# Loading x and the transform matrices before the kernel stage, and taking the first norm's statistics inside it

## The chip, the cores and the metric

The program runs on one core of a Trainium2 chip. The metric is the device time of one execution in microseconds (us), the median of several runs. All data are float32; matrix products of the FFN use the fp32r format (a float32 operand rounded for TensorE) in a split into a high and a low part.

The engines are named as the profile names them: PE (TensorE matrix products), DVE (VectorE), ACT (ScalarE), POOL (GpSimd) and SP (SyncE, here only a queue that issues transfers). Each engine takes its instructions strictly in its own order, and waits on semaphores for the others.

## What is computed

One block of a network with adaptive layer norm (adaLN), a state-space convolution (S4D) and a ReLU feed-forward network (FFN), for 2048 positions of width 576, state size 128, FFN width 4608:

```
sa, ca, ga, sb, cb, gb = silu(c) @ w_mod          # six rows of 576
h  = layernorm(x) * (1 + ca) + sa
K[d, l] = 2 Re sum_n C[d, n] dt[d] exp((-exp(logA) + i A_imag) dt l)
x  = x + ga * (fft_convolution(h, K) + h * D_skip)
h  = layernorm(x) * (1 + cb) + sb
out = x + gb * (relu(h @ w1) @ w2)
```

## The kernel before

**Kernel stage (0 to about 171 us).** `KGen.first` makes the first 512 positions of the convolution kernel K, in six groups of 96 channels (`for g in range(NG)`). Per group ACT takes exponentials and sines of phases that PE made (`exps`, `turns`, `sines`), DVE and POOL build two tables, W2 (32 positions) and W1 (16 positions, by repeated doubling in `doubling`, line 256; the last doubling, m = 8, makes its products on DVE and its sums on POOL), and PE multiplies them (`products`, line 283: 192 small matmuls for each half u of the group, all through the helper of line 62). `rows` (line 325) copies a group's result out of PSUM into `ke` on ACT, and after groups 2 and 5 stores `ke` to DRAM (`kd`, line 403), one half of the channels (p = 0, 1) each. `mod` (line 549) runs between and makes the adaLN rows ga, ca, sa; their weights are loaded on SP at the start (lines 609, 610).

**Conv stage 0 (to about 250 us).** `main` (line 656) opens the pools of what follows and loads the transform matrices fcU, fcK, gc (line 665) on SP. `conv(0)` (line 833) loads x's first 512 rows (line 840), takes the layer norm (`norm1`, `stats`, `norms`: bn_stats, bn_aggr, Sqrt on ACT, reciprocal), and convolves in halves of 288 channels by odd-frequency transforms of length 1024 in four parts: PE multiplies with the matrices (`mm_K` of the kernel, `mm_U` of h; `transform`, line 736; `transform1`, line 774, for the kernel's second half), ACT evicts to Z, DVE does the butterflies (W, then K, U or V), the spectral products Y (`product`, with a temporary T), and PE the inverse (`inverse`, line 925, `ps_i`) added into x on DVE. `load_kt` (line 1023) loads the kernel back from `kd`; the skip term `dsk` is added to its first position (line 857). POOL's queue stores the spectra for later blocks (Rd and Kd of K, Ud of U; line 734). `mod_late` (line 624) makes the rows sb, cb, gb during this stage: for each a load of its weights into the one buffer `wm` on POOL's queue, 25 small matmuls (`mps_sb`, `mps_cb`, `mps_gb`), and for gb a way through DRAM.

**FFN (from about 250 us).** `ffn` (line 1032) runs 4 blocks of 512 positions, each 36 steps over slices of 128 of the FFN width. In block 0 the weights are split into high and low parts (line 1057, 1066 on ACT; 1059, 1069, 1070 on DVE), which are stored in DRAM for the other blocks. Between the matmuls a generator for each block is advanced by a hand-written budget (`step`, `rate`): in block 0 the rest of the kernel positions (`rest`) and conv(1), later conv(2) and conv(3).

**Order.** Python's order is the program's order, but the tile framework plans each engine's queue at build time and may move an instruction that is not marked `keep_in_program_order`. The helpers of `KGen` (`act`, `v`, `stt`, `pool`, `matmul`) mark theirs; the conv stage mostly doesn't. Pools are stacks of SBUF space; a tile in a later pool waits for the last users of the space that it takes over. The 13 transfers at the start and all of `kd`, `W1d`, `W2d`, `Zd` go through SP's queue in order.

Of the kernel before, what the change touches and what calls it, by code (L numbers as in the profile page):

```python
# [10 lines left out]
F32 = mybir.dt.float32  # L11
# [7 lines left out]
P = 128  # L19
# [21 lines left out]
class KGen:  # L41
# [31 lines left out]
    def setup(self, I):  # L73
# [8 lines left out]
        dt = self.pt.tile([P, D], F32, tag="T0", bufs=2, name="dt")  # L82
# [22 lines left out]
        def turn(h):  # L105
            th = self.pt.tile([KR, 4, P], F32, tag="T1", bufs=2, name="th")
# [149 lines left out]
    def doubling(self, g, i, u):  # L256
# [41 lines left out]
    def first(self, setup, mod):  # L298
# [42 lines left out]
        next(mod)  # L341
        turns = self.turns(0)
# [13 lines left out]
        for g in range(NG):  # L356
# [13 lines left out]
            run(double[2])  # L370
            if g + 1 < NG:
# [9 lines left out]
            if g > 0:  # L381
                rows(g - 1)
            run(*double[4:])
# [13 lines left out]
        run(late)  # L397
        return lambda: rows(NG - 1)
# [8 lines left out]
    def rest(self, psum, hs, blocks):  # L407
# [5 lines left out]
        with ExitStack() as ctx:  # L413
            pt = k.pool(ctx, f"kr{hs[0]}{blocks[0]}")
# [91 lines left out]
class Body:  # L506
# [3 lines left out]
    def build(self):  # L510
        nc, tc, I = self.nc, self.tc, self.I
        with ExitStack() as ctx:
# [13 lines left out]
            self.consts()  # L526
            kg = KGen(self)
            with ExitStack() as c2:
                kg.open(c2)
                setup = kg.setup(I)  # L530
                last = kg.first(setup, self.mod(kg))
            self.main(ctx, kg, last)

    def consts(self):
# [11 lines left out]
        self.dsk = c.tile([1, D], F32, name="dsk")  # L546
        nc.gpsimd.dma_start(out=self.dsk, in_=I["dsk"].unsqueeze(0))
# [76 lines left out]
    def mod_late(self):  # L624
# [3 lines left out]
        cb = self.cv.tile([P, 5, 32], F32, name="cb")  # L628
        nc.vector.tensor_copy(cb, self.ct.unsqueeze(2).broadcast_to([P, 5, 32]))
        for i, nm in ((3, "sb"), (4, "cb"), (5, "gb")):  # L630
            w = self.cv.tile([P, 5, D], F32, tag="wm", bufs=1, name=f"wm_{nm}")
# [4 lines left out]
            row = self.cv.tile([P, 2 * P], F32, tag="row", bufs=1, name=f"row_{nm}")  # L636
# [663 lines left out]
```

## Time and profile before

| | |
|---|---|
| time, median of 3 runs | 1431.17 us (1430.52 to 1433.48) |
| span of the profiled execution, first to last instruction | 1432.8 us |
| mean granted PE clock | 0.930 of full |
| PE busy | 1259.9 us (88%), 10720 instructions |
| DVE busy | 888.2 us (62%) |
| ACT busy | 491.2 us (34%) |
| POOL busy | 171.3 us (12%) |
| moved by DMA | 348 MB, 243 GB/s mean |
| first matmul of the FFN (line 1083) | 249.22 us |

A timeline row gives the start, the duration, the engine and line, the operation with the tile it writes and the tiles it reads, the shapes, how many instructions are merged, and in brackets how long the engine stood idle before it and what it waited for. "issue" means that it waited for nothing that the profile shows. A row with SPq or "DMA_DIRECT2D" is the issue of a transfer, not its duration. PE's ends are modelled, so a busy PE is not a PE at its peak.

### The profile page before, as it was taken

The numbers are of one execution on the slowest core, as the hardware profiler recorded it, in microseconds if no ns is written. First come the engines' busy times: TensorE is split into PE (matmuls) and PEld (weight loads), VectorE is DVE, ScalarE is ACT, GpSimd is POOL, SyncE is SP. The second block draws the span as 40 slices with busy tenths as digits, with TensorE's granted clock in tenths as the row PEclk, the third lists the DMA queues.
The fourth block names the chain that finished last, engine by engine and source line by source line (L and its number), as shares of the span: only waits on it lengthen the run. The fifth ranks groups of instructions, "written<-read, shape, count | busy, mean of one in ns | idle before, by whom it ended". The sixth has DMA issues, their size and how long they took to land. (4 is left out here: it accounts for less than half of the span.)

```text
span 1432.8 us, 26177 instructions
## 1 busy us (share of the span) xinstructions
PE 1259.9 (88%) x10720; PEld 994.5 (69%) x10720; DVE 888.2 (62%) x1332; ACT 491.2 (34%) x863; POOL 171.3 (12%) x279
## 2 busy tenths in 40 slices
PE   4665276999988997698999998999999999999997
PEld 2444155777876775476777776778787878888886
DVE  6889388999656678858836688563799532101112
ACT  4777042222221340151224322543332353323321
POOL 0667202000110100011010110010100000000000
PEclk9557588899999998899999999999999999999999
DMA  5647857576597694569867888585889657666662
GB/s 176 249 185 294 296 214 254 192 273 238 188 389 273 234 325 169 204 225 362 277 214 269 333 288 325 158 282 164 332 306 374 196 160 225 196 200 193 197 198 95
DMA packets 120268, 348.21 MB, mean 243 GB/s; under 512 B 23948, under 2 KB 24244, under 8 KB 109140
## 3 DMA queue, kind: packets, MB, share of 16 engines
q1 hardware_dynamic: 101044, 219.44, 46.9%
q0 software_dynamic: 18592, 125.73, 23.2%
q8 instruction: 84, 1.38, 0.4%
q10 hardware_dynamic: 512, 1.38, 0.3%
q14 instruction: 36, 0.29, 0.1%
HBM read 262.73 MB, written 83.76 MB: 242 GB/s over the span
## 5 line engine op out<-in xcount | busy, mean ns | idle before, releaser
L1083 PE MATMUL hps<-xh,w 128*128 128x512 f32 x1152 | 395.4, 402 | 0.0
L1109 PE MATMUL acc<-w,hh 128*128 128x512 f32 x1152 | 371.0, 404 | 8.7 <-DMA w<-L2d 5.7
L1089 DVE SCALAR_TENSOR_TENSOR hl<-hps,hh 128x512 fp32r<-128x512 f32 x144 | 99.0, 687 | 336.8 <-ACT hh L1088 336.5
L1109 PEld LDWEIGHTS acc<-w,hh 128*128 128x128 f32 x1152 | 217.3, 190 | 58.7 <-DMA w<-L2d 6.6
L1083 PEld LDWEIGHTS hps<-xh,w 128*128 128x128 f32 x1152 | 219.4, 191 | 48.2 <-ACT xh L1015 0.4
L1109 PE MATMUL acc<-w,hl 128*128 128x512 f32 x576 | 227.1, 406 | 8.6 <-DVE hl L1089 8.6
L1083 PE MATMUL hps<-xl,w 128*128 128x512 f32 x576 | 233.7, 406 | 0.0
L1088 ACT ACTIVATE hh<-hps 128x512 fp32r<-128x512 f32 x144 | 86.0, 597 | 361.7 <-PE hps L1083 348.3
L1066 ACT ACTIVATE w<-r 128x576 fp32r<-128x576 f32 x144 | 98.9, 687 | 261.3 <-issue 168.5
L1109 PEld LDWEIGHTS acc<-w,hl 128*128 128x128 f32 x576 | 109.6, 191 | 32.9 <-DVE hl L1089 9.5
L1083 PEld LDWEIGHTS hps<-xl,w 128*128 128x128 f32 x576 | 110.4, 192 | 23.6
L1057 ACT ACTIVATE w<-r 128x640 fp32r<-128x640 f32 x144 | 105.4, 732 | 28.4 <-DMA L1d<-w 23.8
L1083 PE MATMUL hps<-xs,w 128*128 128x512 f32 x288 | 99.7, 416 | 13.2 <-DMA w<-L1d 9.3
L62 PE MATMUL kps<-W,W 128*32 128x16 f32 x2304 | 45.6, 219 | 56.5 <-POOL W L59 33.1
L462 PEld LDWEIGHTS kps<-W1r,W2r 128*32 128x32 f32 x3456 | 68.0, 146 | 37.7 <-issue 27.8
L462 PE MATMUL kps<-W1r,W2r 128*32 128x48 f32 (+2 forms) x3456 | 78.3, 237 | 12.6 <-issue 10.2
L62 PEld LDWEIGHTS kps<-W,W 128*32 128x32 f32 x2304 | 40.7, 150 | 68.6 <-POOL W L59 36.1
L919 DVE TENSOR_TENSOR Y<-Y,T 128x1152 f32<-128x1152 f32 x64 | 84.6, 1349 | 0.0
L1083 PEld LDWEIGHTS hps<-xs,w 128*128 128x128 f32 x288 | 54.3, 192 | 27.9 <-DMA w<-L1d 11.0
L744 ACT ACTIVATE Z<-ps_f 128x288 f32<-128x288 f32 x120 | 48.2, 412 | 70.7 <-PE ps_f L743 63.6
L1109 PE MATMUL acc<-hh,w 128*128 128x512 f32 x144 | 58.1, 403 | 10.9 <-DVE w L1069 10.9
L1214 POOL DMA_DIRECT2D out_dram<-x x16 | 8.6, 544 | 463.3 <-DVE x L1206 461.4
(213 smaller groups left out, 1573.6 us busy)
## 6 DMA issues: line engine op xcount, KB each, us to landing
r<-in_w_dram SPq DMA_DIRECT2D x144, 320.0 KB
r<-in_w_dram SPq DMA_DIRECT2D x144, 288.0 KB, 3.4
w<-L1d SPq DMA_DIRECT2D x108, 320.0 KB, 3.8
w<-L2d SPq DMA_DIRECT2D x108, 288.0 KB
W2r<-W2d POOLq DMA_DIRECT2D x18, 1536.0 KB, 8.5
W2d<-W SPq DMA_DIRECT2D x12, 1536.0 KB, 8.6
Ua<-Ud POOLq DMA_DIRECT2D x15, 1152.0 KB, 10.1
W<-W1d POOLq DMA_DIRECT2D x18, 768.0 KB, 9.6
```

Source lines behind the costliest of these rows:

```text
L62: self.tc.keep_in_program_order(self.nc.tensor.matmul(*args, **kw))
L462: nc.tensor.matmul(ps[32 * dd : 32 * dd + 32, q, :], W2[:, r, :, ch], W1[:, :, r, ch], start=(r == 0), stop=(r == 1),)
L744: ev = nc.scalar.activation(Z[:, n2, c], ps[:, :PC], AF.Copy)
L919: v(y, y, T, op=op or ALU.add)
L1057: nc.scalar.activation(w[:, 0], r, AF.Copy)
L1066: nc.scalar.activation(w[:, 0:D], r, AF.Copy)
L1083: nc.tensor.matmul(ps, a, x, start=(i == 0), stop=(i == 13))
L1088: nc.scalar.activation(hh, ps, AF.Relu)
L1089: nc.vector.scalar_tensor_tensor(hl, ps, 0.0, hh, op0=ALU.max, op1=ALU.subtract)
L1109: nc.tensor.matmul(acc[i], a, x, start=(f == 0 and seen[i] == 1), stop=(f == NF - 1 and seen[i] == (3 if i < 4 else 2)),)
L1214: self.nc.gpsimd.dma_start(out=ov[:, n2], in_=x2[:, n2])
```

## The change

- `early` is new. Its first step loads x's first 512 rows, fcK, fcU and gc on SP right behind the adaLN weights of the start. Then, in groups 1 to 4 of the kernel stage, it takes the statistics of one of the four row sets each on DVE (two bn_stats and one bn_aggr, kept in order); in group 5 one Sqrt for all four on ACT (kept), and `moments`, a reciprocal and a product on DVE (not kept).
- `first` returns the second half of group 5's products and the last `rows` as separate pieces; `conv(0)` puts the transform of the kernel's first half (`mm_K(0)`) ahead of them, then `shift`, then the rows.
- `shift` replaces `norm1` in conv(0): ACT normalizes (Identity with scale and bias), then 1 + ca is multiplied and sa added, row set 3 on POOL, the others on DVE.
- The skip term of conv(0) is added on POOL.
- Pools: the kernel stage's lie on the right side of SBUF, the long-lived ones (x, matrices, FFN) on the left; T0, T1, t move from the pool `kg_t` to `kg_c`; conv 0 has a second pool `cvl` for its later tiles; the pools of `rest` and of the later conv stages are on the right too. PSUM pools are opened in the other order.
- fcKn and gcn are issued at step 36 in place of 40.

The core of the diff:

```diff
@@ -64,8 +64,8 @@
-        self.pa, self.pc, self.pt, self.pw = (pool(f"kg_{x}") for x in "actw")
-        self.ps, self.ph = pool("kg_ps", space=PSUM), pool("kg_ph", space=PSUM)
+        self.pt, self.pa, self.pc, self.pw = (pool(f"kg_{x}", side="right") for x in "tacw")
+        self.ph, self.ps = pool("kg_ph", space=PSUM), pool("kg_ps", space=PSUM)
...
@@ -267,10 +267,10 @@
-            t = self.pt.tile([P, 16 * H], F32, tag="T0", bufs=2, name="T0")
-            T = self.pt.tile([P, 16 * H], F32, tag="T1", bufs=2, name="T1")
+            t = self.pc.tile([P, 16 * H], F32, tag="T0", bufs=2, name="T0")
+            T = self.pc.tile([P, 16 * H], F32, tag="T1", bufs=2, name="T1")
-            t = self.pt.tile([P, 8 * H], F32, tag="t", bufs=2, name="t")[:, : 2 * n * m * H]
+            t = self.pc.tile([P, 8 * H], F32, tag="t", bufs=2, name="t")[:, : 2 * n * m * H]
@@ -339,6 +339,8 @@
         next(setup)
         next(mod)
+        early = k.early()
+        next(early)
         turns = self.turns(0)
         next(turns)
         next(setup)
@@ -368,6 +370,8 @@
             run(*double[:2])
             next(mod, None)
             run(double[2])
+            if 0 < g < 5:
+                next(early)
             if g + 1 < NG:
                 turns = self.turns(g + 1)
                 for _ in range(2):
@@ -380,6 +384,8 @@
                 run(late, double[3])
             if g > 0:
                 rows(g - 1)
+            if g + 1 == NG:
+                next(early)
             run(*double[4:])
             for u in range(2):
                 nc.sync.dma_start(
@@ -394,8 +400,9 @@
             run(a)
             if g + 1 < NG:
                 run(sines(g + 1))
-        run(late)
-        return lambda: rows(NG - 1)
+            else:
+                run(early)
+        return late, lambda: rows(NG - 1)
     def store(self, s, p, ke, eng):
...
@@ -524,12 +531,48 @@
             self.L1d = [dr.tile([P, 640], F32, name=f"L1d_{f}") for f in range(NF)]
             self.L2d = [dr.tile([P, D], F32, name=f"L2d_{f}") for f in range(NF)]
             self.consts()
+            self.x2, self.xT, self.ended = {}, {}, -1
+            self.dsk = self.cst.tile([1, D], F32, name="dsk")
+            nc.gpsimd.dma_start(out=self.dsk, in_=I["dsk"].unsqueeze(0))
+            self.sm = self.pool(ctx, "sm")
+            self.x2p = [self.pool(ctx, "x2a")]
             kg = KGen(self)
             with ExitStack() as c2:
                 kg.open(c2)
                 setup = kg.setup(I)
-                last = kg.first(setup, self.mod(kg))
-            self.main(ctx, kg, last)
+                late, last = kg.first(setup, self.mod(kg))
+            self.main(ctx, kg, late, last)
+
+    def early(self):
+
+        nc, I, sm = self.nc, self.I, self.sm
+        x2 = self.x2[0] = self.x2p[0].tile([P, 4, D], F32, tag="x2", bufs=1, name="x2_0")
+        nc.sync.dma_start(out=x2, in_=I["x"][0:512, :].rearrange("(m n) d -> m n d", n=4))
+        self.fcU, self.fcK, self.gc = (
+            sm.tile([P, 4, 2, P], F32, name=n) for n in ("fcU", "fcK", "gc")
+        )
+        for t, n in ((self.fcK, "fck"), (self.fcU, "fcu"), (self.gc, "gc")):
+            nc.sync.dma_start(out=t, in_=I[n])
+        kept = self.tc.keep_in_program_order
+        self.mv1 = mv = sm.tile([P, 4, 5], F32, name="mv1")
+        for i in range(4):
+            yield
+            st = sm.tile([P, 2, 6], F32, tag="st", bufs=8, name="st0")
+            for p in range(2):
+                kept(nc.vector.bn_stats(out=st[:, p], in_=x2[:, i, p * PC : (p + 1) * PC]))
+            kept(nc.vector.bn_aggr(out=mv[:, i, 0:2], in_=st))
+        yield
+        kept(nc.scalar.activation(mv[:, :, 2], mv[:, :, 1], AF.Sqrt, bias=self.eps))
+        yield
+        self.moments(mv)
+        yield
+
+    def moments(self, mv):
+
+        self.nc.vector.reciprocal(mv[:, :, 3], mv[:, :, 2])
+        self.nc.vector.scalar_tensor_tensor(
+            mv[:, :, 4], mv[:, :, 0], -1.0, mv[:, :, 3], op0=ALU.mult, op1=ALU.mult
+        )
     def consts(self):
         nc, I, c = self.nc, self.I, self.cst
...
@@ -625,15 +666,15 @@
-        cb = self.cv.tile([P, 5, 32], F32, name="cb")
+        cb = self.cvl.tile([P, 5, 32], F32, name="cb")
-            w = self.cv.tile([P, 5, D], F32, tag="wm", bufs=1, name=f"wm_{nm}")
+            w = self.cvl.tile([P, 5, D], F32, tag="wm", bufs=1, name=f"wm_{nm}")
-            row = self.cv.tile([P, 2 * P], F32, tag="row", bufs=1, name=f"row_{nm}")
+            row = self.cvl.tile([P, 2 * P], F32, tag="row", bufs=1, name=f"row_{nm}")
@@ -653,37 +694,32 @@
             self.tc.tile_pool(name=name, bufs=1, reuse_waits="tile", **kw)
         )
-    def main(self, ctx, kg, last):
+    def main(self, ctx, kg, late, last):
         nc, tc, I = self.nc, self.tc, self.I
-        self.sm = self.pool(ctx, "sm")
         for n, w in (("sb", 5), ("cb", 5), ("gb", D)):
             self.m[n] = self.sm.tile([P, w], F32, name=f"m_{n}")
-        self.fcU, self.fcK, self.gc = (
-            self.sm.tile([P, 4, 2, P], F32, name=n) for n in ("fcU", "fcK", "gc")
-        )
-        for t, n in ((self.fcU, "fcu"), (self.fcK, "fck"), (self.gc, "gc")):
-            nc.sync.dma_start(out=t, in_=I[n])
-        self.x2p = [self.pool(ctx, "x2a")]
         self.ff = self.pool(ctx, "ff")
         self.xp = [self.pool(ctx, "xa")]
-        self.x2 = {}
-        self.xT = {}
-        self.ended = -1
         with ExitStack() as c:
             self.cps = self.pool(c, "cps0", space=PSUM)
-            self.cv = self.pool(c, "cv0")
-            self.last_rows, self.nps = last, 4
-            self.fcKn, self.gcn = (self.cv.tile([P, 4, P], F32, name=n) for n in ("fcKn", "gcn"))
-            late = None
-            for i, _ in enumerate(self.conv(0)):
-                if i == 40:
+            self.cv = self.pool(c, "cv0", side="right")
+            self.cvl = self.pool(c, "cvl", side="right")
+            self.nps = 4
+            mods = None
+            for i, w in enumerate(self.conv(0)):
+                if w == "late":
+                    for _ in late:
+                        pass
+                elif w == "rows":
+                    last()
+                if i == 36:
                     for t, a in zip((self.fcKn, self.gcn), I["neg"]):
                         nc.gpsimd.dma_start(out=t, in_=a)
                 if i == 60:
-                    late = self.mod_late()
+                    mods = self.mod_late()
                 if i > 60 and i % 6 == 0:
-                    next(late, None)
-            for _ in late:
+                    next(mods, None)
+            for _ in mods:
                 pass
         self.nps = 1
         self.cps = self.pool(ctx, "cps", space=PSUM)
...
@@ -820,26 +854,44 @@
             yield from self.stats(
                 lambda i: x2[:, i, p * PC : (p + 1) * PC], [t[:, p] for t in st]
             )
-        rs = self.norms(st, kept)
+        rs = self.norms(st)
         yield 2.0
-        if kept:
-            self.last_rows()
         for i in range(4):
             mv = rs[i]
             f(h[:, i], x2[:, i], mv[:, 0:1], self.m["ca"], op0=ALU.subtract, op1=ALU.mult)
             f(h[:, i], h[:, i], mv[:, 3:4], self.m["sa"], op0=ALU.mult, op1=ALU.add)
             yield 1.6
+    def shift(self, x2, h):
+
+        nc, mv = self.nc, self.mv1
+        for i in (0, 2, 1, 3):
+            nc.scalar.activation(
+                h[:, i], x2[:, i], AF.Identity, scale=mv[:, i, 3:4], bias=mv[:, i, 4:5]
+            )
+        for i in (0, 2, 1, 3):
+            v = (nc.gpsimd if i == 3 else nc.vector).tensor_tensor
+            v(h[:, i], h[:, i], self.m["ca"], op=ALU.mult)
+            v(h[:, i], h[:, i], self.m["sa"], op=ALU.add)
+            yield 1.6
+
     def conv(self, s):
         nc = self.nc
         v = nc.vector.tensor_tensor
         xp = self.xp[s % 2]
-        x2 = self.x2p[s % 2].tile([P, 4, D], F32, tag="x2", bufs=1, name=f"x2_{s}")
-        self.x2[s] = x2
-        (nc.gpsimd if s else nc.sync).dma_start(
-            out=x2, in_=self.I["x"][s * 512 : (s + 1) * 512, :].rearrange("(m n) d -> m n d", n=4)
-        )
+        if s:
+            x2 = self.x2p[s % 2].tile([P, 4, D], F32, tag="x2", bufs=1, name=f"x2_{s}")
+            self.x2[s] = x2
+            nc.gpsimd.dma_start(
+                out=x2,
+                in_=self.I["x"][s * 512 : (s + 1) * 512, :].rearrange("(m n) d -> m n d", n=4),
+            )
+        else:
+            x2 = self.x2[0]
+            self.fcKn, self.gcn = (
+                self.cv.tile([P, 4, P], F32, name=n) for n in ("fcKn", "gcn")
+            )
         kt = [self.load_kt(s, 0), None]
         yield -1
         yield -1
@@ -854,7 +906,8 @@
             ktv = kt[p].rearrange("p (t dd g) q -> p t dd g q", t=2, g=2)
             if s == 0:
                 dv = self.dsk.rearrange("o (dd p q) -> o dd p q", dd=4, p=2)[:, :, p]
-                v(ktv[0:1, 0, :, 0], ktv[0:1, 0, :, 0], dv, op=ALU.add)
+                k0 = ktv[0:1, 0, :, 0]
+                nc.gpsimd.tensor_tensor(k0, k0, dv, op=ALU.add)
             src = lambda n2: ktv[:, n2 // 2, :, n2 % 2]
             if s == 0 and p == 1:
                 return self.transform1(src, self.fcK, self.fcKn, Z)
@@ -953,10 +1006,12 @@
         Us, Ks, Vs = [], [], []
         ZK, ZU = self.spec("Z"), None
         if s == 0:
-            yield from self.norm1(x2, h, True)
             yield from mm_K(0, ZK)
+            yield "late"
+            yield from self.shift(x2, h)
+            yield "rows"
         else:
-            yield from both(self.norm1(x2, h, False), mm_K(0, ZK))
+            yield from both(self.norm1(x2, h), mm_K(0, ZK))
         kt[1] = self.load_kt(s, 1)
         ZU = self.spec("Z")
         yield from both(spec_K(0, ZK), mm_U(0, ZU))
...
```

The built order of the changed kernel around the end of the kernel stage, each engine's own queue (names shortened, repeats merged; in the kernel before, the four Sqrt stood in the same place on ACT, and Rd, Kd of K_1 came after wm_cb on POOL):

```
ACT : ... ke (group 4) | table load | Sqrt | Z | h0 | Z Z Z | h2 | Z Z Z Z | h1 h3 | ke (group 5) | Z ...
DVE : ... T (group 5, first doubling) | reciprocal | W W | product of the moments | t T | W W | ... | T T T T |
      h0 h0 | W | h2 | W | h2 | h1 | W | h1 | W | K_0 | W W W W | U_0 | W W W W | T T | copy | six FFN splits |
      U_1 | Y_0 | V_0 | K_1 | x x | Y_1 ...
PE  : ... group 4 | group 5, u = 0 | mm_K(0) | group 5, u = 1 | mm_U(0) | mm_U(1) | mm_K(1) | inverse (one output) |
      mps_sb | inverse (three outputs) | mps_cb | mps_gb | second inverse ...
POOL: ... zs zs | fcKn gcn | four sums of group 5 | skip term | h3 h3 | Rd_0 Kd_0 | Ud_0 | skip term | wm_sb |
      Ud_1 | Rd_1 Kd_1 | wm_cb | wm_gb | gb's way through DRAM | rest: W, Z, W2 loads (x of conv(1) behind the third W)
SP  : ... wm_sa | x fcK fcU gc | ... | Zd Zd | kt | W1d W1d | r | kd kd | r r | kt | r ...
```

Further on the order of conv(1)'s DVE work in FFN block 0 differs: its bn_stats stand some 60 instructions earlier, ahead of the last kernel positions of `rest`, and in its first spectral product an `hl` (line 1089) stands between two of the steps where before it stood behind the inverse butterflies.

More of the change, by code (lines that the diff above doesn't have):

```diff
@@ L105, in turn @@
         def turn(h):
-            th = self.pt.tile([KR, 4, P], F32, tag="T1", bufs=2, name="th")
+            th = self.pc.tile([KR, 4, P], F32, tag="T1", bufs=2, name="th")
             dtb = dtT[:, h].unsqueeze(2).broadcast_to([KR, 4, P])
@@ L413, in rest @@
         with ExitStack() as ctx:
-            pt = k.pool(ctx, f"kr{hs[0]}{blocks[0]}")
+            pt = k.pool(ctx, f"kr{hs[0]}{blocks[0]}", side="right")
             def load(h):
@@ L545, in consts @@
         nc.gpsimd.dma_start(out=self.sgn, in_=I["sgn"])
-        self.dsk = c.tile([1, D], F32, name="dsk")
-        nc.gpsimd.dma_start(out=self.dsk, in_=I["dsk"].unsqueeze(0))
     def mod(self, kg):
@@ L694, in pool @@
         def pool(s):
-            self.cv = self.pool(self.cvs, f"cv{s}")
+            self.cv = self.cvl = self.pool(self.cvs, f"cv{s}", side="right")
         def block0():
@@ L725, in half @@
     def half(self, name):
-        return self.cv.tile([P, 4, PC], F32, tag="T", bufs=2, name=name)
+        return self.cvl.tile([P, 4, PC], F32, tag="T", bufs=2, name=name)
     def load(self, src, name):
@@ L792, in stats, with norms @@
             yield 0.45
-    def norms(self, st, kept):
+    def norms(self, st):
         nc = self.nc
@@ L800, in norms @@
             nc.vector.bn_aggr(out=mv[:, 0:2], in_=st[i])
-            sq = nc.scalar.activation(mv[:, 2:3], mv[:, 1:2], AF.Sqrt, bias=self.eps)
-            if kept:
-                self.tc.keep_in_program_order(sq)
+            nc.scalar.activation(mv[:, 2:3], mv[:, 1:2], AF.Sqrt, bias=self.eps)
             rs.append(mv)
@@ L813, in sums, with norm1 @@
         return [self.sm.tile([P, 2, 6], F32, tag="st", bufs=8, name=name) for _ in range(4)]
-    def norm1(self, x2, h, kept):
+    def norm1(self, x2, h):
         f = self.nc.vector.scalar_tensor_tensor
@@ L985, in conv @@
             )
-        rs = self.norms(st, False)
+        rs = self.norms(st)
         yield 2.0
-        h2 = [self.cv.tile([P, D + 64], F32, tag="h2", bufs=4, name="h2") for _ in range(4)]
+        h2 = [self.cvl.tile([P, D + 64], F32, tag="h2", bufs=4, name="h2") for _ in range(4)]
         for n2 in range(4):
```

5 lines of the change are left out of this document (2 added, 3 removed).

## The prediction

> **What bounds the kernel now.** I read the page first, then busy time by stretches, then the timeline from 125 to 260 us, then what PE waited for after that.
>
> ```profile
> 150.00:172.00 22.00, 6.64 (x382) 6.25 (x382) 0.40 (x2) 0.00 (x0) 4.80 (x7) 0.50 1.02 348
> 350.00:400.00 50.00, 50.00 (x563) 40.35 (x554) 31.29 (x39) 12.25 (x21) 6.85 (x13) 1.00 0.65 231
> 550.00:600.00 50.00, 37.50 (x132) 28.56 (x132) 38.91 (x55) 7.41 (x12) 2.63 (x5) 0.84 0.69 247
> 1200.00:1300.00 100.00, 100.00 (x443) 82.83 (x442) 12.88 (x20) 30.20 (x48) 1.88 (x4) 1.00 0.70 207
> ```
>
> Columns: stretch, its length, busy time of PE, PE weight loads, DVE, ACT, POOL, then the granted clock, DMA share, GB/s. Once the FFN runs, PE is nearly full (100 of 100 us late, 37.5 of 50 at worst), so a microsecond by which the FFN starts earlier is a microsecond of the end. Between 150 and 172 no engine works: DVE 0.4 us, PE 6.6, while the DMA engines are full at 348 GB/s. That hole is what the change aims at.
>
> ```profile
> 145.29 0.70 PE L62 MATMUL kps<-W,W 128*32 128x16 f32 x31 [1.86 <-issue]
> 149.62 0.30 PE L62 MATMUL kps<-W,W 128*32 128x16 f32 x2 [3.63 <-POOL W L59]
> 150.57 1.66 PE L62 MATMUL kps<-W,W 128*32 128x16 f32 x94 [0.66 <-POOL W L59]
> 156.02 2.14 PE L62 MATMUL kps<-W,W 128*32 128x16 f32 x127 [3.79 <-issue]
> 164.24 2.13 PE L62 MATMUL kps<-W,W 128*32 128x16 f32 x128 [6.08 <-issue]
> 170.44 0.70 PE L62 MATMUL kps<-W,W 128*32 128x16 f32 x33 [4.06 <-issue]
> 172.62 2.98 DVE L791 BATCH_NORM_STATS2 st<-x 128x6 f32<-128x288 f32 x8 [22.22 <-DMA x<-in_x_dram]
> 176.50 0.47 ACT L50 ACTIVATE ke<-kps 128x384 f32<-128x384 f32 x1
> 181.97 5.64 PE L743 MATMUL ps_f<-kt,fcK 128*128 128x288 f32 x16 [10.82 <-DVE kt L857]
> 187.45 2.83 PE L743 MATMUL ps_f<-h,fcU 128*128 128x288 f32 x11
> ```
>
> Three things end late: x (DVE waits 22.22 us), the last kernel products (PE done at 171.1, idle 13.9 us of that for nothing but the next instructions, about every 128 products), and the transform of K, which waits behind the norm on DVE.
>
> **The change, part by part.** *x and matrices early.* The four loads queue on SP behind wm_sa, the last adaLN weight of the start, long before their use. The 22.22 us wait goes. Fewer bytes are in flight after 150, so I price PE's idle at an instruction block at 2.0 us, near the 1.86 of the row at 145.29, with 3.8 to 6.1 as the other end. At the front the loads follow the weights in their queue; I cost them nothing.
>
> *Statistics in the kernel stage.* In each of four row groups two bn_stats and one aggregate, which I count as a third: 3 x 2.98/8 = 1.1 us of DVE, ahead of the wait shown here:
>
> ```profile
> 127.89 0.96 DVE L53 TENSOR_TENSOR k<-ph,k 128x768 f32<-128x768 f32 x1 [1.14 <-ACT k L50]
> ```
>
> 1.14 us of idle for ACT's k cover it: nothing. Without that cover it would be 4 x 1.1 = 4.5.
>
> *The moments.* This is the catch. The Sqrt follows ke of group 4 on ACT. The built order puts the reciprocal that reads it into DVE's doubling chain, right behind the first T.
>
> ```profile
> 140.88 0.36 DVE L53 TENSOR_TENSOR T<-W,Zp 128x192 f32<-128x192 f32 x1
> 141.28 0.42 DVE L53 TENSOR_TENSOR W<-t,T 128x96 f32<-128x96 f32 x2
> 146.06 0.49 ACT L50 ACTIVATE ke<-kps 128x384 f32<-128x384 f32 x1 [7.24 <-PE kps L62]
> 146.56 1.28 ACT L801 ACT_TABLE_LOAD   x1
> 146.63 3.54 DVE L53 TENSOR_TENSOR T<-W,Zp 128x768 f32<-128x768 f32 x4
> 148.57 3.88 POOL L59 TENSOR_TENSOR W<-T,T 128x384 f32<-128x384 f32 x4 [1.60 <-issue]
> 48.54 1.28 ACT L50 ACT_TABLE_LOAD   x1
> 49.83 0.81 ACT L50 ACTIVATE s<-k 128x768 f32<-128x768 f32 x1
> ```
>
> ke ends at 146.55, the table at 147.84, Sqrt near 148.1: DVE stands from 141.2 to 148.1. That is 6.9 us, with two small operations 7.2. Queued behind are all of group 5's doublings, POOL's last sums and the last products. POOL ends at 152.45 + 7.2 = 159.6.
>
> [...]
>
> *Kernel products and transform of K reordered.* PE starts at 149.62 + 7.2 = 156.8, ends the block of 94 at 159.4, idles 2.0, does the other 96 (1.7) until 163.1, then the K transform (5.64) until 168.8, whose kt now gets its skip term on POOL. Then 192 products of the second half, 3.4 us, and one more 2.0 idle (the other boundary passes under the transform): 174.1. ke follows at 174.2, 2.3 us before the old 176.50. The shift runs meanwhile on ACT, DVE and POOL. Its slowest part is row 3 on POOL, two 128x576 at 3.88/4 x 1.5 = 1.5 us each; ACT delivers it near 171, so it ends by 174. So the U transform starts at 174.1 in place of 187.45.
>
> [...]
>
> *DVE from there.*
>
> ```profile
> 192.25 0.75 DVE L757 TENSOR_TENSOR W<-Z 128x576 f32<-128x576 f32 x1
> 211.94 0.74 DVE L757 TENSOR_TENSOR V<-Y 128x576 f32<-128x576 f32 x1
> 217.06 0.44 DVE L771 TENSOR_TENSOR K<-Z 128x288 f32<-128x288 f32 x1
> 233.73 0.68 DVE L1070 TENSOR_TENSOR w<-r,w 128x512 fp32r<-128x512 f32 x1
> ```
>
> The first W of U needs four outputs, eight passes at 2.83/11 us and an eviction: some 2.8 us (an estimate), so 176.9. From that W to the first V took 19.7 us of full DVE. Now one skip sum leaves it (0.4, as wide as the row at 217.06), five more of the six first FFN weight splits move into it (at 0.68 each at most 3.4; two are an eighth as wide as the row at 233.73, so 2.2) with a small copy (0.3), and the second W pair waits some 0.4 for PE: 22.2, so V at 199.1 against 211.94 and K_1 done at 204.7 against 217.43. DVE is 12.7 us ahead.
>
> *What is late next: the adaLN weights.* They use one buffer, each load waiting for the products of the one before, and PE's second inverse transform is queued behind the third product.
>
> ```profile
> 210.41 0.77 POOL L609 DMA_DIRECT2D wm_cb<-in_w_mod_dram  x1 [5.92 <-PE mps_sb L619]
> 217.56 2.22 PE L619 MATMUL mps_cb<-wm_cb,cb 128*32 128x128 f32 x50 [1.13 <-DMA wm_cb<-in_w_mod_dram]
> 217.79 0.57 POOL L734 DMA_DIRECT2D Rd<-K  x1 [6.08 <-DVE K L771]
> 220.08 0.77 POOL L609 DMA_DIRECT2D wm_gb<-in_w_mod_dram  x1 [1.18 <-PE mps_cb L619]
> 230.03 3.86 PE L619 MATMUL mps_gb<-wm_gb,cb 128*32 128x128 f32 x50 [3.31 <-DMA wm_gb<-in_w_mod_dram]
> 233.82 5.32 PE L940 MATMUL ps_i<-V,gc 128*128 128x288 f32 x16
> 249.22 0.73 PE L1083 MATMUL hps<-xs,w 128*128 128x512 f32 x2 [1.54 <-ACT xf L1013]
> ```
>
> Before, wm_cb went out ahead of the stores Rd and Kd and took 7.1 us, and wm_gb behind them landed 12.2 us after Rd's issue. In the new order Rd and Kd of K_1 stand ahead of wm_cb on POOL, so wm_cb pays that 12.2 (and some 0.6, since mps_sb now runs after the first inverse output): 204.8 + 12.8 = 217.6. mps_cb takes 3.86 after such an idle (2.22 warm): 221.5. wm_gb 7.1: 228.7. mps_gb 3.86: 232.6. The second inverse starts at 232.7 against 233.82. With both products warm and mps_sb too it is 229.4. The stage gains 1.1 to 4.4; I take 1.2, the cold end, since PE idles over 4 us ahead of each and mps_gb was cold after 3.31. From there to 249.22 nothing changes: PE paces the tail.
>
> *Block 0 of the FFN.* conv(1)'s x now stands far earlier in POOL's queue, and its statistics on DVE ahead of idle like that at 475.31.
>
> ```profile
> 475.31 0.23 DVE L1069 TENSOR_TENSOR w<-r,w 128x64 fp32r<-128x64 f32 x1 [5.52 <-ACT w L1066]
> 482.40 2.97 DVE L791 BATCH_NORM_STATS2 st<-x 128x6 f32<-128x288 f32 x8
> 548.14 0.79 PE L1109 MATMUL acc<-hh,w 128*128 128x512 f32 x1 [6.24 <-DVE w L1069]
> 601.93 2.08 PE L1109 MATMUL acc<-w,hl 128*128 128x512 f32 x4 [8.64 <-DVE hl L1089]
> 265.07 0.53 POOL L421 DMA_DIRECT2D W<-W1d  x1 [19.55 <-DVE T L431]
> ```
>
> Some 3.4 us of DVE leave the busy stretch, and in the first product an hl now comes between its steps. PE stood 6.24 and 8.64 us for DVE there. The gain lies between 0 and 14.9; I take 3, near the work moved. The early load of that x sits in POOL's queue between two kernel loads, where POOL was waiting 19.55 us for DVE: nothing, or a few us without that slack.
>
> **Sum.** 1.2 + 3.0 = 4.2 less. The profiled execution spans 1432.8, which becomes 1428.6. The span is 1.6 above the median of the three runs, so the median 1431.17 becomes 1427.0.
>
> **Rivals.** (1) The wait is only swapped: the weights hold the second inverse to its old time and block 0 keeps its stalls (they hang on the length of the spectral products on DVE, which stays). 1430.5, within 0.2%. For it: the second product's order is unchanged. (2) The weights aren't late: PE warm and wm_cb shares the DMA engines with the stores instead of queueing behind them, 7.1 again. Then wm_cb lands at 214.8, mps_gb ends near 226.4, and the stage gains 7; with 3 from block 0, 1421. For it: the rows give 7.1 where a load runs alone; against it, the DMA engines had no room while Rd, Kd and wm_gb ran:
>
> ```profile
> 220.00:225.00 5.00, 4.79 (x20) 3.58 (x21) 3.56 (x5) 0.53 (x4) 1.30 (x2) 1.00 1.04 361
> ```
>
> (3) Slower: PE's idle at the instruction blocks stays at 3.8 to 6.1 as at 156 to 170, because W2d, W1d and kt still fill the queues. Then the products of the second half end 4 to 6 us after 174.1, and U, V, K_1 and the weights behind them follow one for one. It decides from 175.3 on, where the 1.2 us are used up; at 180 the stage loses 4.7, and without block 0's gain that is 1436. Against it: the gap was 1.86 before the loads began.
>
> **How the numbers follow.** Forecast 0.42 (own range 1423.5 to 1430), rival 1 0.22, rival 2 0.18, rival 3 0.18. A change under 0.2%, 2.9 us, can't be told from none: faster means below 1428.3, slower above 1434.0. Faster: 0.32 of the forecast's 0.42 and rival 2, 0.50. Same: 0.10, 0.20 of rival 1 and 0.02 of rival 3, 0.32. Slower: 0.02 of rival 1 and 0.16 of rival 3, 0.18. The range 1419 to 1436 holds rival 2 with room and rival 3 to its price.
>
> **What would show it.** A DVE wait of about 7 us for ACT's Sqrt near 141 us. PE's last kps product between 173 and 177. The first W of U near 177. wm_cb landing 10 us or more after its issue, PE waiting for wm_cb and wm_gb, and the second inverse at 230 to 234. First hps within 4 us of 249. PE stalls at the first product of conv(1) below 6 us. Wrong if the reciprocal doesn't wait, if the second inverse starts before 228 or after 236, or if block 0's length changes by more than 8 us.

## The result, and the profile after

| | before | changed |
|---|---|---|
| median, first comparison (9 runs each) | 1433.73 us | 1428.51 us, ratio 0.9969 (0.9954 to 0.9983) |
| median, second comparison (27 and 12 runs) | 1433.36 us | 1430.23 us, ratio 0.9980 (0.9961 to 0.9999) |
| span of the profiled executions | 1432.8, 1434.0, 1433.0 us | 1423.3, 1428.5 us |

The change makes the kernel faster by 3 to 5 us (5.2 and 3.1 between the medians; forecast 1427.0); both intervals end below 1, the second only just. The first profile of the changed kernel is the fastest of its nine runs, so its span alone would overstate the gain. The busy time by stretches, same columns as for before:

```profile
150.00:172.00 22.00, 13.81 (x407) 11.64 (x408) 13.86 (x22) 7.07 (x15) 7.19 (x7) 0.67 0.63 185
550.00:600.00 50.00, 35.64 (x135) 27.30 (x134) 38.08 (x51) 8.64 (x14) 2.63 (x5) 0.88 0.67 244
```

The hole at 150 to 172 us is in good part filled (DVE 0.40 to 13.86 us, PE 6.64 to 13.81) and the DMA engines have room there (share 1.02 to 0.63). What became of that shows in the timeline of the changed kernel:

```profile
147.31 0.18 DVE L572 RECIPROCAL mv<-mv 128x4 f32<-128x4 f32 x1 [6.57 <-ACT mv L565]
...
155.68 0.30 PE L62 MATMUL kps<-W,W 128*32 128x16 f32 x2 [10.58 <-POOL W L59]
...
160.16 1.66 PE L62 MATMUL kps<-W,W 128*32 128x16 f32 x96 [1.86 <-issue]
...
167.18 3.14 PE L62 MATMUL kps<-W,W 128*32 128x16 f32 x192
...
169.89 1.97 DVE L875 TENSOR_TENSOR h<-h,m_sa 128x576 f32<-128x576 f32 x1
...
170.24 8.05 PE L779 MATMUL ps_f<-h,fcU 128*128 128x288 f32 x32
...
171.32 1.80 POOL L875 TENSOR_TENSOR h<-h,m_sa 128x576 f32<-128x576 f32 x1
...
171.78 1.96 DVE L794 TENSOR_TENSOR W<-Z 128x576 f32<-128x576 f32 x1
...
176.48 0.75 DVE L793 TENSOR_TENSOR W<-Z 128x576 f32<-128x576 f32 x1
...
182.88 5.01 POOL L910 TENSOR_TENSOR kt<-kt,dsk 1x288 f32<-1x288 f32 x1
...
198.72 0.76 DVE L793 TENSOR_TENSOR V<-Y 128x576 f32<-128x576 f32 x1
...
206.15 0.77 POOL L650 DMA_DIRECT2D wm_cb<-in_w_mod_dram  x1 [0.50 <-PE mps_sb L660]
...
216.84 3.86 PE L660 MATMUL mps_cb<-wm_cb,cb 128*32 128x128 f32 x50 [6.04 <-DMA wm_cb<-in_w_mod_dram]
...
221.00 0.80 POOL L650 DMA_DIRECT2D wm_gb<-in_w_mod_dram  x1 [13.55 <-PE mps_cb L660]
...
227.33 3.86 PE L660 MATMUL mps_gb<-wm_gb,cb 128*32 128x128 f32 x50 [5.49 <-DMA wm_gb<-in_w_mod_dram]
...
231.12 6.64 PE L993 MATMUL ps_i<-V,gc 128*128 128x288 f32 x16
...
246.93 1.22 PE L1138 MATMUL hps<-xs,w 128*128 128x512 f32 x2 [1.54 <-ACT xf L1068]
```

The U transform starts 17.2 us earlier (187.45 to 170.24), the first V 13.2 us earlier (211.94 to 198.72), the second inverse only 2.7 us (233.82 to 231.12), the first FFN product 2.3 us. DVE's waits in this stage (line, tile, releaser: us, times, longest), which were 22.2 us for x before:

```profile
DVE x L998 <- PE ps_i L993: 15.6, 4, 13.9
DVE h L874 <- ACT h L869: 8.0, 1, 8.0
DVE mv L572 <- ACT mv L565: 6.6, 1, 6.6
```

Much of the wait was exchanged for three others: Sqrt, ACT's normalized rows, and the second inverse behind the adaLN weights.

### The profile page after: what moved, and what is told of

It is laid out like the page before. It is cut to its first block, busy times and chain, and to the rows that moved or that the text cites. A ratio compares the mean times of both kernels' runs of the same rounds, so it can differ in the third digit from the quotient of the medians.

```text
span 1423.3 us, 26160 instructions
## 1 busy us (share of the span) xinstructions
PE 1261.6 (89%) x10720; PEld 994.9 (70%) x10720; DVE 889.7 (63%) x1322; ACT 494.2 (35%) x864; POOL 180.8 (13%) x283
## 4 chain that ended last, share of the span: by engine, by line
PE 66%; DVE 10%; DMA 6%; issue 3%; ACT 1%; POOL 1%; SPq 0%; POOLq 0%; DVEq 0%; ACTq 0%
PE acc L1164 28%; PE hps L1138 27%; PE kps L469 4%; PE ps_f L779 3%; DMA w<-L2d 2%; PE ps_i L993 2%; DVE Y L972 2%; DVE T L970 2%; DVE T L438 1%; DMA L1d<-w 1%; DVE W1r L440 1%; DMA wm_cb<-in_w_mod_dram 1%; DVE W1r L444 1%; DMA Ua<-Ud 1%; DMA Ud<-U 1%
## 5 line engine op out<-in xcount | busy, mean ns | idle before, releaser
L1138 PE MATMUL hps<-xs,w 128*128 128x512 f32 x288 | 100.8, 419 | 10.3 <-DMA w<-L1d 3.2
```

The lines of the kernel that those rows point to most:

```text
L1138: nc.tensor.matmul(ps, a, x, start=(i == 0), stop=(i == 13))
```

## The experiments

The kernel stage ran up to 2.4 us apart in executions with the same order up to there, so the table counts from the first T of 768 columns of group 4 on DVE (110.67 to 113.38 us from the start). The expected texts give times from the start of the span, mostly on the clock of the changed kernel's first profile (112.98); where the difference decides between two theories, the text below says so. Blocks 1 to 3 run from the first output copy of block 0 to that of the last block. Ratios are against the kernel before, run beside each.

| kernel | first V | second inverse | first FFN product | block 0, us | blocks 1 to 3, us | ratio (95%) |
|---|---|---|---|---|---|---|
| before, 3 profiles | 98.6, 98.6, 99.6 | 120.4, 120.4, 121.3 | 135.8, 135.8, 137.1 | 372.6, 373.5, 374.5 | 798.9, 799.8, 797.4 | |
| changed, 2 profiles | 85.7, 86.3 | 118.1, 118.8 | 134.0, 134.0 | 372.3, 373.8 | 792.3, 795.9 | 0.9969, 0.9980 |
| moments kept | 84.9 | 117.0 | 131.2 | 373.8 | 791.8 | 0.9936 (0.9916 to 0.9956) |
| two buffers wm | 86.0 | 109.1 | 125.2 | 373.0 | 796.5 | 0.9891 (0.9874 to 0.9908) |
| both | 84.3 | 107.7 | 123.5 | 372.9 | 794.7 | 0.9895 (0.9873 to 0.9917) |
| both, POOL's steps on DVE | 81.7 | 104.5 | 120.0 | 374.7 | 797.5 | 0.9879 (0.9863 to 0.9896) |
| only POOL's steps on DVE | 82.1 | 120.2 | 135.7 | 374.1 | 793.9 | 0.9969 (0.9953 to 0.9985) |
| early load alone | 88.2 | 116.9 | 130.6 | 372.1 | 798.1 | 0.9952 (0.9935 to 0.9969) |
| kept, kt early | 84.7 | 117.0 | 131.3 | 376.5 | 796.7 | 0.9959 (0.9940 to 0.9977) |
| two buffers, POOL's steps on DVE | 82.4 | 104.2 | 120.8 | 374.6 | 794.5 | 0.9876 (0.9846 to 0.9907) |
| all edits | 82.7 | 104.6 | 121.3 | 378.3 | 795.1 | 0.9882 (0.9854 to 0.9910) |

**The moments kept in program order.**

```diff
-        self.nc.vector.reciprocal(mv[:, :, 3], mv[:, :, 2])
-        self.nc.vector.scalar_tensor_tensor(
+        kept = self.tc.keep_in_program_order
+        kept(self.nc.vector.reciprocal(mv[:, :, 3], mv[:, :, 2]))
+        kept(self.nc.vector.scalar_tensor_tensor(
...
```

> The two moments operations behind the Sqrt are kept in program order, so they stand on DVE behind group 5's last doubling and not in front of it; nothing else moves. Theory A (the 6.57 us stall lies on the path): DVE no longer waits at 147, POOL's sums, the last products, U, V and K_1 come some 6.5 us earlier, and the adaLN weights with them, since wm_cb is issued when mps_sb is done and mps_sb follows the first inverse: second inverse at 224 to 225.5 (231.1 in the changed kernel), first hps near 240.5, median near 1422. Rival B (the weights' chain is held by the DMA engines and not by K_1): second inverse not before 229, gain under 2 us. Rival C (PE's idle at instruction blocks comes back because W2d, W1d and kt still fill the queues): gain 2 to 4 us.

The stall is gone, yet the second inverse comes only 1.1 to 1.8 us earlier by the table. The timeline of this kernel shows what was late next:

```profile
154.31 1.66 PE L62 MATMUL kps<-W,W 128*32 128x16 f32 x96 [4.90 <-issue]
...
156.85 0.78 POOL L911 TENSOR_TENSOR kt<-kt,dsk 1x288 f32<-1x288 f32 x1 [7.20 <-DMA kt<-kd]
157.68 0.85 PE L780 MATMUL ps_f<-kt,fcK 128*128 128x288 f32 x1 [1.71 <-POOL kt L911]
```

PE's idle at the instruction block (the texts' name for the idles marked "issue" between the kernel products, 127 or 128 products apart in the kernel before; here the one ahead of the 96 products) rose from 1.86 to 4.90 us, and the load kt landed after that, so that PE waited another 1.71 us. Theory A falls. B is half right: the inverse stands at 227.66, but this kernel stage ran 2.3 us ahead of the changed kernel's, and on that kernel's clock it is 230.0 (112.98 + 117.0), not before 229, with a gain at the inverse of under 2 us. Its reason doesn't hold, since the chain of weights moved with the first V (0.8 to 1.4 us earlier). C's size, 2 to 4 us, holds in the first FFN product (2.7 us). The second inverse itself took 4.15 us here, in place of 6.64 and 5.04 in the two profiles of the changed kernel.

**Two buffers wm.**

```diff
-            w = self.cvl.tile([P, 5, D], F32, tag="wm", bufs=1, name=f"wm_{nm}")
...
+            ws[nm] = self.cvl.tile([P, 5, D], F32, tag="wm", bufs=2, name=f"wm_{nm}")
...
+        load(3, "sb")
+        load(4, "cb")
...
+            if nm == "sb":
+                load(5, "gb")
```

> Two buffers wm: wm_sb and wm_cb are both issued at the old place of wm_sb, wm_gb when mps_sb is done; order on PE, DVE and ACT unchanged. Theory A (the one-buffer chain of the adaLN weights caps the change): mps_cb no longer waits, wm_gb lands near 217, the second inverse starts when V_1 and mps_gb are there, near 221 (231.1 in the changed kernel), first hps near 237, median near 1418.5. Rival D (what the stage gains is lost again in block 0 of the FFN, which is bound there by its own transfers and DVE): first hps near 237 too, but block 0 longer by what was gained and the median within 3 us of 1428.5. Rival E (the transfers are slow because the DMA engines are full, not because of the order): wm_gb lands after 224 and the second inverse is after 228.

```profile
209.15 2.22 PE L660 MATMUL mps_cb<-wm_cb,cb 128*32 128x128 f32 x50
...
216.43 3.86 PE L660 MATMUL mps_gb<-wm_gb,cb 128*32 128x128 f32 x50 [4.12 <-DMA wm_gb<-in_w_mod_dram]
220.22 6.47 PE L1002 MATMUL ps_i<-V,gc 128*128 128x288 f32 x16
```

In this kernel's timeline mps_cb no longer waits and the second inverse starts at 220.22, as theory A had it; 9.0 to 9.7 us earlier by the table, of which 8.8 reach the first FFN product (134.0 to 125.2). D and E fall. The chain of weight loads was what held the change. The edit does two things to that chain, which this run doesn't tell apart: wm_cb need not wait for wm_sb's products, and it is issued ahead of the stores Rd and Kd of K_1.

**Both.**

> Both edits, the kept moments and the two buffers wm. Theory A: the gains add, second inverse near 214.5, first hps near 230.5, median near 1412. Rival D: stage earlier by 16 us, time by less than 5. Rival E: no better than the better of the two alone.

The gains do not add: 107.7 against 109.1, ratio no better. With two buffers wm_gb becomes the limit (PE waited 4.45 us for it here), and the stall's removal is again met by a 5.45 us idle at the instruction block. A is refuted in its sum, and of the rivals E's forecast is the nearer.

**POOL's two steps back on DVE.** First on top of both edits, then alone, then with the two buffers alone.

```diff
-            v = (nc.gpsimd if i == 3 else nc.vector).tensor_tensor
+            v = nc.vector.tensor_tensor
...
-                nc.gpsimd.tensor_tensor(k0, k0, dv, op=ALU.add)
+                (nc.vector if p else nc.gpsimd).tensor_tensor(k0, k0, dv, op=ALU.add)
```

> As with both edits, and the two steps that the change gave to POOL while DVE is busy are back on DVE: row set 3 of shift and the skip term of the kernel's second half. Theory F (DVE and POOL slow each other: DVE's 128x576 sums took 1.97 in place of 0.75 us, POOL's 1x288 add 5.01 in place of 0.78): DVE's first W of K takes 0.75 each, the rows cost DVE 1.5 + 0.4 and save 2.4, wm_sb is issued some 4 us earlier against K_1; 0.5 to 1.5 us less than with both edits. Rival: row set 3 comes later to PE, since DVE makes it last, and the U transform starts later: 1 to 2 us more.

> The changed kernel with row set 3 of shift and the skip term of the kernel's second half back on DVE, nothing else. Theory F (DVE and POOL slow each other while both read two operands from SBUF): no 1.9 us sums on DVE near 170, wm_sb issued near 183 in place of 187.85, the transform of the kernel's second half starts before 184 in place of 187.95; of that only DVE's part is on the path, so second inverse 0.5 to 2.5 us earlier (229 to 230.5), median 0.5 to 2.5 us below the changed kernel. Rival (row set 3 comes later from DVE than it came from POOL and holds PE's U transform): second inverse 0 to 2 us later.

> Row set 3 and the second skip term on DVE, and two buffers wm; the moments not kept, so that the Sqrt stall of 6.6 is there. Theory A (the one-buffer chain of weights is what ate the 5.4 us that V_0 had gained with the two steps back on DVE): V_0 near 193.5, second inverse near 216 in place of 231.8, and the kept moments on top (second inverse 216.2 in that run) are then worth next to nothing, since kt's load is late without the stall; median 1416 to 1419. Rival: second inverse 220 as with the two buffers alone.

Alone, the first V comes 3.7 to 4.3 us earlier, but the second inverse 1.4 to 2.1 us later. Theory F's premise holds in the times (near 170 two sums of h took 1.42 us together here and that of W 0.75, none 1.9), its gain at the inverse doesn't; the rival's time is met, but not by its reason, since U's transform started no later. The timeline of this kernel:

```profile
193.65 0.74 DVE L793 TENSOR_TENSOR V<-Y 128x576 f32<-128x576 f32 x1
...
215.88 0.80 POOL L650 DMA_DIRECT2D wm_gb<-in_w_mod_dram  x1 [13.17 <-PE mps_cb L660]
...
227.99 3.86 PE L660 MATMUL mps_gb<-wm_gb,cb 128*32 128x128 f32 x50 [11.26 <-DMA wm_gb<-in_w_mod_dram]
231.78 5.42 PE L993 MATMUL ps_i<-V,gc 128*128 128x288 f32 x16
```

wm_gb was issued 5.1 us earlier than in the changed kernel (221.00; 3.7 earlier counted from group 4) and took 12.0 us in place of 6.2, while loads and stores of the first FFN weights, which DVE now split earlier, ran beside it (1.84 MB on the queue q1 between 205 and 236 us, none in the changed kernel between 206 and 232). With two buffers the same two steps are worth 4.9 us at the second inverse (109.1 to 104.2), near theory A's 216 (216.96), and on top of both edits 3.2 (107.7 to 104.5), more than F's 0.5 to 1.5: with the first V 3.6 us earlier wm_gb is issued earlier too, and PE has it 10.3 us after its issue in place of 11.9. And the kept moments on top of that give nothing (104.5): the 6.6 us stall, the first number of my working, has no price in that setting.

**The early load alone.** The statistics, reciprocal and h stand as one piece on DVE behind the last doubling, with Sqrt on ACT between them; ACT's shift and POOL's row set 3 fall away.

```diff
+            yield from self.norm1(x2, h, True)
             yield from mm_K(0, ZK)
             yield "late"
-            yield from self.shift(x2, h)
```

> x and the matrices loaded early as in the changed kernel, with its pools and order of products, but the statistics and the norm are taken on DVE behind group 5's doublings, as one piece in program order (as before the change, there behind the wait for x); ACT's shift, POOL's row set 3 and the Sqrt ahead of the doublings fall away. Theory G (the early load alone brings the gain, and statistics in the kernel stage bring a stall of 6.6 and the wait for ACT's h of 8.0 with them): h is done on DVE near 161, the U transform starts at 165 to 168 in place of 170.2, first W of U near 171 in place of 176.5, second inverse near 225, median near 1423. Rival H (statistics and norm, 10 us of DVE, now stand on the path): second inverse 231 or later, median 1428 or more.

Theory G's times were too early (U transform 168.81, second inverse 229.47, median 1426.67), rival H's too late, and the first V even comes 2 us later than in the changed kernel. Still this kernel is no slower than the whole change, and its second inverse is 1.2 to 1.9 us earlier. Its timeline shows what moved:

```profile
204.90 0.77 POOL L639 DMA_DIRECT2D wm_cb<-in_w_mod_dram  x1 [8.37 <-PE mps_sb L649]
...
206.64 0.57 POOL L759 DMA_DIRECT2D Rd<-K  x1 [0.45 <-DVE K L796]
...
212.25 3.86 PE L649 MATMUL mps_cb<-wm_cb,cb 128*32 128x128 f32 x50 [6.74 <-DMA wm_cb<-in_w_mod_dram]
...
225.27 2.22 PE L649 MATMUL mps_gb<-wm_gb,cb 128*32 128x128 f32 x50
```

Here mps_sb runs ahead of the first inverse, so wm_cb is issued ahead of Rd and Kd and PE has it 7.4 us later (10.7 in the changed kernel); mps_gb waits for nothing. The first inverse, behind mps_cb now, starts 17.2 us later (216.81, 199.58). So this kernel is no slower without the statistics inside the kernel stage and without the shift on ACT; but since POOL's and PE's orders differ too, what those parts are worth by themselves stays open.

**kt issued in group 4** (with the kept moments; gc is loaded later to make room).

```diff
+            if i == 3:
+                self.kt0 = self.load_kt(0, 0, sm)
...
+                    nc.gpsimd.dma_start(out=self.gc, in_=I["gc"])
```

> The kept moments, and the load kt of the kernel's first half (kt<-kd, 288-byte pieces) issued on SP in group 4, about 25 us earlier, in place of behind group 5's W2d and Zd; to make room gc is loaded on POOL's queue after the U transform and lies with the rows sb, cb, gb in a later pool. Order on PE, DVE and ACT in conv stage 0 as with the kept moments alone. Theory K (with the Sqrt stall gone the next late thing was kt, which landed 10.5 us after its issue and held POOL's skip term to 156.85): skip term near 151, transform of K at 153 to 156 in place of 157.68, U transform at 162.4 to 165.4 in place of 167.13, second inverse 223 to 226 in place of 227.66. Theory L (PE's idle at the instruction block is what holds it, kt would come in time): idle ahead of the 96 products stays at 4.9, transform of K at 156 or later, second inverse at 226 or later. If the idle falls below 2.5, kt's small pieces were what made it long. Block 0: the statistics of conv(1) stand where they stood before the change; Theory M (their place is worth nothing): block 0 372 to 375 us again.

```profile
149.04 0.30 PE L62 MATMUL kps<-W,W 128*32 128x16 f32 x2 [2.79 <-POOL W L59]
...
151.84 0.78 POOL L916 TENSOR_TENSOR kt<-kt,dsk 1x288 f32<-1x288 f32 x1
...
156.27 1.66 PE L62 MATMUL kps<-W,W 128*32 128x16 f32 x96 [4.61 <-issue]
157.85 5.91 PE L783 MATMUL ps_f<-kt,fcK 128*128 128x288 f32 x16
...
188.78 0.23 DVE L1132 TENSOR_TENSOR w<-r,w 128x64 fp32r<-128x64 f32 x1 [2.49 <-ACT w L1129]
```

kt was in time, as K said, and the 1.71 us wait is gone; the 4.61 us at the instruction block stayed, as L said. K's times are on the clock of the kept moments' profile, whose kernel stage ran 2.1 us ahead of this one. Counted from group 4 the transform of K came 2.0 us earlier than there (47.0 to 45.1) and the transform of U 2.3 (56.5 to 54.1), both within K's range. By the first V the gain is gone (84.9, 84.7): DVE stood 2.49 us for an FFN weight that ACT splits, queued ahead of it, which it had not done with the kept moments alone. K's second inverse fell with that (117.0 in both). The DMA view of that idle (queue: packets, MB, share of 16 engines), first for this kernel between 151.7 and 156.2 us, then for the changed kernel in its own short idle, 158.3 to 160.1 us:

```profile
q1 hardware_dynamic: 1178, 0.95, 73.9%
q0 software_dynamic: 159, 0.52, 29.3%
q8 instruction: 1, 0.02, 1.4%
```

```profile
q1 hardware_dynamic: 127, 0.69, 96.7%
```

The long idle holds one packet of the instruction queue, which starts between 153.8 and 154.0. The short one holds none: there the packet starts between 157.4 and 157.6, while PE is still at the products before. In both PE took up its work 2.3 to 2.8 us behind the start of the packet, so the length of the idle goes with the lateness of the packet: it started 1.7 to 1.9 us behind the first of the 96 products ahead of the idle (155.68) in the changed kernel, 4.8 to 5.0 behind it (149.04) here. Why it was late isn't shown. Full DMA engines alone don't tell the two apart, since they were full in the short idle too (96.7%), and emptying them was not tried. Block 0 was 376.5 us, outside the 372 to 375 of theory M, but it is one profile and other transfers moved too, so what the place of conv(1)'s statistics is worth stays open.

**All edits.**

> All together: kept moments, early kt, two buffers wm, row set 3 and second skip term on DVE. Theories A and K: second inverse 211 to 214 (216.2 without the early kt), first hps near 228, median 1412 to 1415. Rival (wm_gb, issued when mps_sb is done and 10 to 12 us under way, holds the second inverse): 216 or later, nothing gained.

Further profiles of both kernels were taken for blocks 1 to 3 (the first two texts count them to the end of the span, 811.0 and 804.1 in the first profiles; the third counts as the table does):

> The kernel before once more, for a second profile. Theory N (the blocks of the FFN behind block 0 vary from execution to execution and owe nothing to the change): from the first to the last block's end 803 to 809 us, as in the profiles of the changed kernel and its variants (803.6 to 809.2), in place of the 811.0 of the first profile. Theory S (the change shortens them): 810 or more again. Block 0 itself 372 to 375 us by both.

> The changed kernel once more: second profile and a tighter interval. Ratio 0.995 to 0.998; second inverse 229 to 233; Theory N: blocks 1 to 3 differ by several us from the 804.1 of the first profile; Theory S: within 1 us of it.

> The kernel before, third profile. Theory N (blocks 1 to 3 vary by execution): from the first to the last block's output below 798; Theory S (the change shortens them, the eight profiles with its FFN gave 791.8 to 798.1): 798.5 to 800 again, as 798.9 and 799.8.

All edits together bring nothing over the two buffers with POOL's steps on DVE (104.6 against 104.2), as the rival had it; their one profile has the longest block 0 of the fourteen (378.3). The five versions with two buffers (0.9876 to 0.9895) can't be told apart by their intervals; each gains about three to six times what the change itself did (0.9969, 0.9980), and two buffers alone do it with one edit.

To the span's end the second profiles gave 811.9 and 807.7: S for the kernel before, N for the changed one, which differs by 3.6 from its first. By the table blocks 1 to 3 last 797.4 to 799.8 us in three profiles of before and 791.8 to 798.1 in eleven with the changed FFN part; the third profile of before is below 798, as N had it, and the ranges overlap. On the mean that is 3.5 us less (798.7 and 795.2), but profiles with the same FFN part lie 6.3 us apart. The traces say where: between the output copies of blocks 1 and 3 all fourteen take 484.1 to 487.0 us, and the difference lies in block 1 alone (312.0 to 315.5 before, 307.3 to 314.0 in the others). In block 1 PE stood 12.1 to 13.9 us for loads of the weights w in the three profiles of before, 9.3 and 14.0 in the two of the changed kernel, so these waits scatter in one and the same kernel. No run isolates a cause: it stays open whether the change shortens block 1.

## Why the prediction was right, step by step

The size was right, and the main step too, but of the sum's two terms one was not where the prediction put it.

- *Sqrt stall.* 6.9 forecast, 6.57 measured. That it counts in full, as the sum took it, holds only while it stands: without it 4.8 of its 6.6 us returned at the instruction block (3.0) and at kt (1.7).
- *Last products.* Forecast to end at 174.1, ended at 170.3. Mis-sized: of two idles of 2.0 at instruction blocks one was 1.86 and the other did not come (192 products in one piece), and the 94 products ahead of them ended 1.1 us before the forecast. The start of the U transform was 3.9 us early with it.
- *First W of U.* 176.9 forecast, 176.48 measured, by luck: PE was early, but DVE was busy with W and K until then, as two of its sums took 1.97 and 1.96 us beside POOL's row set 3. The prediction had POOL's two steps at 1.5 us each (1.88 and 1.80 measured) and no price for DVE beside them. The first V (199.1, 198.72) and K_1's store (204.8, 204.59) follow.
- *The weights.* mps_cb at 216.84 (217.6 forecast), mps_gb at 227.33 (228.7), second inverse at 231.12 (232.7). This was the step that mattered, and the two buffers show it: 9 us. Counted from group 4 the second inverse came 2.2 us earlier on the mean (120.7 to 118.5) against 1.2 forecast.
- *Block 0.* The step that failed: "The gain lies between 0 and 14.9; I take 3". The gain was 0.5 us, within the scatter, 373.5 before and 373.0 changed on the mean. The waits of PE in block 0, before and then changed, say where it went:

```profile
PE acc L1109 <- DVE w L1069: 10.9, 4, 6.2
PE acc L1109 <- DVE hl L1089: 8.6, 1, 8.6
...
PE acc L1109 <- DVE w L1070: 2.7, 2, 2.5
...
PE hps L1083 <- DVE w L1059: 0.4, 1, 0.4
```

```profile
PE acc L1164 <- DVE hl L1144: 13.3, 3, 8.6
...
PE acc L1164 <- DVE w L1124: 4.9, 2, 2.5
...
PE hps L1138 <- DVE w L1114: 2.6, 2, 2.2
...
PE acc L1164 <- DVE w L1125: 0.4, 2, 0.2
```

PE waits 8.3 us less for w at the two acc lines (13.6 to 5.3) and 6.9 us more for hl and for w at hps (9.0 to 15.9). The longest stall, for the hl of the second product, stayed as it was (8.64, 8.65). The work moved on DVE, as forecast, and the same DVE was late with the next tile.

- *Not foreseen.* The rest of the gain, as far as the scatter lets it be told, stands in block 1, where nothing was forecast. So rival 1 was right about block 0 and wrong only by 2 us about the second inverse; that the sum came out is luck, since a term that was missing, and may be scatter, made up for one that was not there. Rival 3's idle came in the runs with the moments kept (4.6 to 5.5 us), though no run shows that full queues made it; with the Sqrt stall in place it was 1.6 to 1.9. Rival 2's price for wm_cb, 7.1, is what the early load alone shows (7.4), where wm_cb goes ahead of the stores and not beside them.

## What to carry to other kernels

When a long wait is taken away, follow the next serial resource to its end before polishing the piece itself: here a one-buffer chain of loads took 10 of 13 us, and a second buffer was worth more than the whole change. A stall that shows 6.6 us has the price of the distance to the next late thing, and an experiment that removes it alone does not give that price in another setting. An edit that saves DVE time should be read at the point where the stage is held; four us at the first V were worth nothing until the weights were out of the way. And times of two profiles are compared from a common point ahead of the edit: two microseconds of scatter before it can make a theory look right or wrong.

## What the runs showed of the hardware

Steps of DVE and POOL that ran beside each other took longer in the changed kernel. DVE's two 128x576 sums beside POOL's steps of row set 3 (1.88 and 1.80 us) took 1.97 and 1.96 us in place of 0.75, and POOL's 1x288 add took 5.01 us beside a run of DVE operations, 0.78 us where DVE stood. That one small add lasted through several of DVE's operations (182.88 to 187.89), and DVE's 128x576 sums beside it stayed at 0.74 and 0.75. With row set 3 on DVE and POOL idle there, two sums of h took 1.42 together and that of W 0.75. Why the two slow each other isn't shown, nor that it hangs on operands in SBUF.

PE's idle ahead of the 96 products was 1.6 to 1.9 us in the kernels with the Sqrt stall and 4.6 to 5.7 in those without, all at the same place. In five profiles without the stall (moments kept, both, both with POOL's steps on DVE, early load alone, kept with kt early) the idle holds one packet of the instruction queue; in four with it (changed, two buffers, only POOL's steps on DVE, two buffers with POOL's steps on DVE) it holds none. The idle ends 2.3 to 2.8 us behind the packet's start in the changed kernel and with kt early, and each of the three idles of 3.79, 6.08 and 4.06 us in the kernel before ends 2.2 to 2.6 us behind one. The packet starts 1.7 to 1.9 us behind the first of the 96 products ahead in the changed kernel, 4.8 to 5.0 with kt early; what makes it late stays open.
